# VectorE takes every score-decay product of the first twelve attention steps

## The chip, the cores and the metric

One core of one Trainium2 chip runs the whole kernel. The metric is the device time of one execution in microseconds (us); of several runs the median counts.

## The reference

A chunked linear attention with decay, then two feed-forward layers on its output. Cut to what matters:

```
for each chunk of the sequence:
    L = exp(cum_i - cum_j) * causal          # decays
    M = (C @ B.T) * L                        # scores times decays
    y = M @ x + (C @ state) * exp(cum)
    state = decay_full * state + sum(B x decay_from_j)
x = y, heads side by side                    # 3072 tokens x 256
x = max(x@w1, x@w2, x@w3) @ w_out            # hidden 768
out = (sigmoid(x@w_gate) * (x@w_val)) @ w_out2   # hidden 1536
```

The change touches the product `M`, the scores times the decays.

## The kernel before, in words

Attention is 64 steps: eight chunks c of 96 positions, and in each chunk eight groups g of four (batch, head) pairs; step k is c*8+g. A step makes its scores on TensorE (L280 for the first sixteen steps, L283 after) into a PSUM tile `s`, multiplies them by the decays into an SBUF tile `mt` (five buffers, used in turn), and multiplies that by `x` (L301) into a PSUM tile `y`, which also holds the state. The 16 state columns of `mt` are made by GpSimd (L288). The product itself is made in one of two ways: VectorE reads PSUM and writes `mt` (L295), or ScalarE copies PSUM to `mt` (L291) and GpSimd multiplies there (L292). After four steps ScalarE and VectorE evict `y` as a rounded high part and a low part (L310, L312) and VectorE transposes the state (L316).

A decay tile `dec` serves two steps; it has four buffers, is loaded by SyncE (L213) and turned into running products by two VectorE scans (L235). The load of tile n+4 into the buffer of tile n waits until both steps of tile n have used it.

The first feed-forward layer takes 512 tokens at a time (`t`). Twelve steps must be done for the first. Per hidden block m of 128 there are three products (`u_t_m_0`, `u_t_m_1`, `u_t_m_2`, six matmuls each, L350 to L352) in three PSUM banks, which they share with the scores `s`. ScalarE copies the first out (L395), VectorE takes the maximum with the second and the third (L397, L399), ScalarE and GpSimd split the result into `hi` and `lo` (L388, L390), and TensorE multiplies these into `o`. A bank is free for the next score or product only when it was read.

The weights of the first layer come as twelve loads named `raw_a00`, `raw_a01`, `raw_a10` to `raw_a51` (block, part). Each is decoded when it has landed: ScalarE L141, L144, L143, VectorE L148, L150, ScalarE L155, GpSimd L157. Most of these loads stand on SyncE's queue behind the load of a decay tile.

The order on each engine is not the written one. A scheduler with a timeline of its own sorts the instructions of each engine when the program is built; on the chip each engine then takes them in that order. So an edit of one step can move instructions of others.

Of the kernel before, what the change touches and what calls it, by code (L numbers as in the profile page):

```python
# [40 lines left out]
START = 12  # L41
# [25 lines left out]
def scan_attention_then_ffn(ctx: ExitStack, tc: tile.TileContext, xh, ah, bch, pick, bn, w1, w2, w3,  # L67
# [201 lines left out]
    def attention(k, ahead):  # L269

        c, g = steps[k]
        m = mt[k % MTS]
        if k < FIRST:
            ck = cm[:, k % MASKED]
            act.mul(ck.rearrange("p q i -> p (q i)"), bcf[c][:, BW:], pk[:, g:g + 1])
        ps = psu.tile([128, 4, 128], F32, tag="up", name=f"s{c}_{g}")
        for q in range(4):
            u = 4 * g + q
            if k < FIRST:
                pe.matmul(ps[:, q, 0:CH], bcf[c][:, 128 * q:128 * q + 128], ck[:, q],  # L280
                          start=True, stop=True)
            else:
                pe.matmul(ps[:, q, 0:CH], bi[c % 2][:, u, :], cs[c][:, u, :],  # L283
                          start=True, stop=True)
        for _ in range(ahead + 1):
            yield
        dc = dec[k // 2][:, 4 * (g % 2):4 * (g % 2) + 4]
        pool.tensor_tensor(out=m[:, :, CH:CH + N], in0=bx[c][:, 4 * g:4 * g + 4, :],  # L288
                           in1=dc[:, :, CH:LW].to_broadcast([128, 4, N]), op=ALU.mult)
        if k >= 4 and k % 2 == 0:  # L290
            act.copy(m[:, :, 0:CH], ps[:, :, 0:CH])  # L291
            pool.tensor_tensor(out=m[:, :, 0:CH], in0=m[:, :, 0:CH], in1=dc[:, :, 1:LW],  # L292
                               op=ALU.mult)
        else:
            last[0] = dve.tensor_tensor(out=m[:, :, 0:CH], in0=ps[:, :, 0:CH], in1=dc[:, :, 1:LW],  # L295
                                        op=ALU.mult)
        prepare(k)
        yield
        y = ys[g // 4]
        for q in range(4):  # L300
            pe.matmul(y[32 * q:32 * q + 32, g % 4, 0:CH + N], xs[c][:, 4 * g + q, :], m[:, q, :],  # L301
                      start=True, stop=True)
        if g % 4 == 3:
            yield
            h = g // 4
            o = (c * CP + 2 * CH * h) % RING
            src = y[:, :, 0:CH].rearrange("p (b k) i -> p b k i", k=KD)
            hi, lo = (v[:, :, o:o + 2 * CH].rearrange("p k (b i) -> p b k i", b=2)
                      for v in (xt_hi, xt_lo))
            act.copy(hi, src)  # L310
            yield
            dve.tensor_tensor(out=lo, in0=src, in1=hi.bitcast(F32), op=ALU.subtract)  # L312
            if c + 1 < NC:
                for q in range(4):
                    rows = slice(32 * q, 32 * q + 32)
                    dve.transpose(  # L316
                        out=xs[c + 1][rows, 16 * h:16 * h + 16, :].rearrange(
                            "p (g q) d -> p g q d", q=4)[:, :, q, :],
                        in_=y[rows, :, CH:128])

    def prepare(k):

        c, g = divmod(k, NG)
        if g == 0 and 0 < c < NC - 1:
            load_x(c + 1)
            splits.append(split_bc(c + 1))
        if splits and next(splits[0], None) is splits:
            splits.pop()
        n = k // 2
        if k % 2 == 0:  # L330
            if 5 <= n + 4 < NC * NP:
                load_decay(n + 4, ad)
        elif k < 9:
            decay(n + 1, n == 0)
        else:
            for i in ([n + 1] if k == 9 else []) + [n + 2]:
                if i < NC * NP:
                    with tc.issue_after(last[0].ins) if k > FIRST else ExitStack():
                        decay(i)

    def att_step(ahead=0):
        pipe.add(attention(done[0], ahead))
        done[0] += 1
# [236 lines left out]
```

## Time and profile before

| | |
|---|---|
| median of 3 runs | 581.4 us (580.17 to 582.3) |
| the profiled execution | 582.93 us |
| its span, first to last instruction | 581.1 us |
| TensorE busy | 560.9 us, 97% of the span |
| VectorE, ScalarE, GpSimd busy | 312.7, 260.7, 197.8 us |

The profiled execution is one run beside the three; 1.83 us of its time lie outside the span. Shares of busy time are means over stages with different limits: the attention start up to about 36 us, the stage in which the first layer's weights are decoded, and the rest.

### The profile page before, as it was taken

The numbers are of one execution on the slowest core, as the hardware profiler recorded it, in microseconds if no ns is written. First come the engines' busy times: TensorE is split into PE (matmuls) and PEld (weight loads), VectorE is DVE, ScalarE is ACT, GpSimd is POOL, SyncE is SP. The second block draws the span as 40 slices with busy tenths as digits, with TensorE's granted clock in tenths as the row PEclk, the third lists the DMA queues.
The fourth block names the chain that finished last, engine by engine and source line by source line (L and its number), as shares of the span: only waits on it lengthen the run. The fifth ranks groups of instructions, "written<-read, shape, count | busy, mean of one in ns | idle before, by whom it ended". The sixth has DMA issues, their size and how long they took to land.

```text
span 581.1 us, 8016 instructions
## 1 busy us (share of the span) xinstructions
PE 560.9 (97%) x2992; PEld 448.7 (77%) x2992; DVE 312.7 (54%) x455; ACT 260.7 (45%) x475; POOL 197.8 (34%) x219
## 2 busy tenths in 40 slices
PE   4988799999999999999999999999999999999997
PEld 4766567677777777788888888888888888888885
DVE  3879995655857754345766664243343333333332
ACT  4677645225344333256967675442333233232322
POOL 3566965427556523234665555310000000000000
PEclk9998999999999999999999999999999999999999
DMA  7999876827875800395000000010000001000000
GB/s 243 335 241 259 222 153 111 174 65 134 196 162 142 156 2 0 94 363 195 2 1 2 0 2 0 1 72 1 1 7 30 1 0 38 0 1 36 1 0 36
DMA packets 35366, 50.52 MB, mean 87 GB/s; under 512 B 3456, under 2 KB 24320, under 8 KB 35328
## 3 DMA queue, kind: packets, MB, share of 16 engines
q1 hardware_dynamic: 35328, 50.02, 33.4%
q8 instruction: 23, 0.38, 0.3%
q14 instruction: 15, 0.12, 0.1%
HBM read 38.51 MB, written 3.25 MB: 72 GB/s over the span
## 4 chain that ended last, share of the span: by engine, by line
PE 87%; DMA 6%; DVE 3%; issue 1%; SPq 1%; ACT 1%; POOL 0%; DVEq 0%; ACTq 0%; POOLq 0%
PE u L350 19%; PE u L351 18%; PE u L352 18%; PE o L351 8%; PE o L350 8%; PE o L352 8%; PE s L280 3%; PE y L301 3%; DMA raw_a<-in_w 3%; PE s L283 1%; DMA dec<-in_ah 1%; DMA cs<-parts 1%; DMA raw_a<-in_wo 1%; DVE dec L235 1%; SPq L252 0%
## 5 line engine op out<-in xcount | busy, mean ns | idle before, releaser
L388 ACT CAST hi<-s 128x512 fp32r<-128x512 f32 x108 | 67.1, 621 | 181.1 <-DVE s L406 132.1
L390 POOL TENSOR_TENSOR lo<-s,hi 128x512 fp32r<-128x512 f32 x60 | 80.9, 1348 | 95.3 <-ACT hi L388 92.3
L350 PE MATMUL u<-xt_hi,w_b 128*128 128x512 f32 x288 | 112.0, 389 | 0.0
L351 PE MATMUL u<-xt_lo,w_b 128*128 128x512 f32 x288 | 112.0, 389 | 0.0
L352 PE MATMUL u<-xt_hi,w_b 128*128 128x512 f32 x288 | 112.0, 389 | 0.0
L406 DVE TENSOR_TENSOR s<-u,s 128x512 f32<-128x512 f32 x72 | 49.6, 689 | 103.8 <-PE u L352 101.7
L350 PE MATMUL u<-xt_hi,w_a 128*128 128x512 f32 x216 | 89.1, 413 | 2.9 <-DVE s L399 2.0
L351 PE MATMUL u<-xt_lo,w_a 128*128 128x512 f32 x216 | 85.5, 396 | 0.1
L352 PE MATMUL u<-xt_hi,w_a 128*128 128x512 f32 x216 | 85.0, 394 | 0.0
L352 PEld LDWEIGHTS u<-xt_hi,w_b 128*128 128x128 f32 x288 | 54.1, 188 | 11.3
L350 PEld LDWEIGHTS u<-xt_hi,w_b 128*128 128x128 f32 x288 | 54.1, 188 | 11.2
L351 PEld LDWEIGHTS u<-xt_lo,w_b 128*128 128x128 f32 x288 | 54.0, 188 | 11.2
L235 DVE TENSOR_TENSOR_SCAN dec<-dec,delta 128x388 f32<-128x388 f32 x64 | 57.9, 945 | 1.7 <-DMA dec<-ad 1.5
L351 PE MATMUL o<-lo,w_b 128*128 128x512 f32 x144 | 56.1, 390 | 0.0
L352 PE MATMUL o<-hi,w_b 128*128 128x512 f32 x144 | 56.0, 389 | 0.0
L350 PEld LDWEIGHTS u<-xt_hi,w_a 128*128 128x128 f32 x216 | 41.2, 191 | 14.7 <-DVE s L399 2.5
L390 DVE TENSOR_TENSOR lo<-s,hi 128x512 fp32r<-128x512 f32 x48 | 33.2, 692 | 32.5 <-ACT hi L388 32.4
L352 PEld LDWEIGHTS u<-xt_hi,w_a 128*128 128x128 f32 x216 | 41.1, 190 | 9.1
L351 PEld LDWEIGHTS u<-xt_lo,w_a 128*128 128x128 f32 x216 | 41.1, 191 | 8.3 <-DVE xt_lo L312 0.6
L404 ACT ACTIVATE s<-u 128x512 f32<-128x512 f32 x72 | 43.1, 599 | 3.6 <-PE u L352 3.0
L350 PE MATMUL o<-hi,w_b 128*128 128x512 f32 x144 | 44.4, 390 | 0.1
L397 DVE TENSOR_TENSOR s<-u,s 128x512 f32<-128x512 f32 x36 | 24.8, 688 | 35.7 <-PE u L352 32.8
(60 smaller groups left out, 769.7 us busy)
## 6 DMA issues: line engine op xcount, KB each, us to landing
dec<-ad SPq DMA_DIRECT2D x30, 388.0 KB, 5.2
raw_a<-in_w SPq DMA_DIRECT2D x18, 256.0 KB, 7.2
bi<-parts SPq DMA_DIRECT2D x36, 128.0 KB, 5.3
cs<-parts SPq DMA_DIRECT2D x36, 96.0 KB, 5.2
xs<-in_xh SPq DMA_DIRECT2D x6, 512.0 KB, 4.5
raw_b<-in_wg SPq DMA_DIRECT2D x12, 256.0 KB, 5.8
raw_b<-in_wv SPq DMA_DIRECT2D x12, 256.0 KB, 5.8
raw_b<-in_wo SPq DMA_DIRECT2D x12, 256.0 KB, 5.8
```

The source lines that it names most:

```text
L235: dve.tensor_tensor_scan(out=f, data0=f, data1=delta.rearrange("p u w -> p (u w)"), initial=0.0, op0=ALU.mult, op1=ALU.add)
L280: pe.matmul(ps[:, q, 0:CH], bcf[c][:, 128 * q:128 * q + 128], ck[:, q], start=True, stop=True)
L283: pe.matmul(ps[:, q, 0:CH], bi[c % 2][:, u, :], cs[c][:, u, :], start=True, stop=True)
L301: pe.matmul(y[32 * q:32 * q + 32, g % 4, 0:CH + N], xs[c][:, 4 * g + q, :], m[:, q, :], start=True, stop=True)
L350: pe.matmul(ps, wlo, a_hi(k), start=k == 0, stop=False)
L351: pe.matmul(ps, whi, a_lo(k), start=False, stop=False)
L352: pe.matmul(ps, whi, a_hi(k), start=False, stop=k == kn - 1)
L388: act.copy(hl[0], s)
L390: eng.tensor_tensor(out=hl[1], in0=s, in1=hl[0].bitcast(F32), op=ALU.subtract)
L397: dve.tensor_tensor(out=s, in0=banks[1], in1=s, op=ALU.max)
L404: evict[0] = act.activation(out=s, in_=banks[0], func=AF.Sigmoid)
L406: evict[1] = dve.tensor_tensor(out=s, in0=banks[1], in1=s, op=ALU.mult)
```

## The change

```diff
-        if k >= 4 and k % 2 == 0:
+        if k >= START and k % 2 == 0:
             act.copy(m[:, :, 0:CH], ps[:, :, 0:CH])
             pool.tensor_tensor(out=m[:, :, 0:CH], in0=m[:, :, 0:CH], in1=dc[:, :, 1:LW],
                                op=ALU.mult)
         else:
             last[0] = dve.tensor_tensor(out=m[:, :, 0:CH], in0=ps[:, :, 0:CH], in1=dc[:, :, 1:LW],
                                         op=ALU.mult)
```

`START` is 12. So the products of steps 4, 6, 8 and 10 become one VectorE instruction each, in place of a ScalarE copy and a GpSimd product. From step 12 on nothing is edited. The built order changes on all five engines in about the first 120 us of the program, and not after it.

GpSimd, around steps 8 to 13. Before: the products of steps 8 and 10 (`mt3`, `mt0`) stand between the state columns of later steps.

```order
L288 TENSOR_TENSOR mt1_99<-bx1_156,dec5_216 128x4x16
L292 TENSOR_TENSOR mt3_101<-mt3_101,dec4_159 128x4x96
L288 TENSOR_TENSOR mt2_100<-bx1_156,dec6_248 128x4x16
L288 TENSOR_TENSOR mt3_101<-bx1_156,dec6_248 128x4x16
L292 TENSOR_TENSOR mt0_98<-mt0_98,dec5_216 128x4x96
L157 TENSOR_TENSOR w_a00_420<-r_a00_409,w_a00_420 128x512
```

The same place on GpSimd in the change:

```order
L288 TENSOR_TENSOR mt1_99<-bx1_156,dec5_216 128x4x16
L288 TENSOR_TENSOR mt2_100<-bx1_156,dec6_247 128x4x16
L157 TENSOR_TENSOR w_a00_416<-r_a00_405,w_a00_416 128x512
L288 TENSOR_TENSOR mt3_101<-bx1_156,dec6_247 128x4x16
L157 TENSOR_TENSOR w_a01_426<-r_a01_412,w_a01_426 128x512
```

Both products are gone, and the first weights' low part stands ahead of the state columns of step 13.

VectorE, around the product of step 17 (`mt2` from `s2_1`), which ends the use of the decay tile `dec8`. Before:

```order
L399 TENSOR_TENSOR s3_0_1_571<-u3_0_1_2_620,s3_0_1_571 128x512
L150 ISA r_a40_495<-t_a40_516,r_a40_495 128x1024
L295 TENSOR_TENSOR mt2_100<-s2_1_668,dec8_332 128x4x96
L235 SCALAR_TENSOR_TENSOR dec10_522<-dec10_522,delta_95 128x388 x2
L312 TENSOR_TENSOR xt_lo_93<-y1_104,xt_hi_92 128x2x2x96
L316 STREAM_TRANSPOSE xs2_324<-y1_104 32x4x32 x4
```

The same place on VectorE in the change:

```order
L150 ISA r_a40_491<-t_a40_512,r_a40_491 128x1024
L397 TENSOR_TENSOR s3_0_1_567<-u3_0_1_1_594,s3_0_1_567 128x512
L399 TENSOR_TENSOR s3_0_1_567<-u3_0_1_2_616,s3_0_1_567 128x512
L148 SCALAR_TENSOR_TENSOR t_a41_558<-raw_a41_520,sg1_88 128x512
L312 TENSOR_TENSOR xt_lo_93<-y1_104,xt_hi_92 128x2x2x96
L316 STREAM_TRANSPOSE xs2_321<-y1_104 32x4x32 x4
L295 TENSOR_TENSOR mt2_100<-s2_1_664,dec8_329 128x4x96
```

The decode of `raw_a41`, a low part and the transposes now stand ahead of the product of step 17.

ScalarE, around the copy of `u_0_3_0` out of its bank (L395 `s3_0_3`). Before:

```order
L388 CAST hi3_0_2_674<-s3_0_2_673 128x512
L395 COPY s3_0_3_769<-u3_0_3_0_772 128x512
L247 CAST parts3_661<-bc3_659 128x896
L291 COPY mt0_98<-s2_4_787 128x4x96
L155 CAST w_a50_650<-r_a50_616 128x512
L141 ACTIVATE sg1_88<-raw_a51_665 128x512
L144 ACTIVATE r_a51_706<-raw_a51_665 128x512
```

The same place on ScalarE in the change:

```order
L388 CAST hi3_0_2_670<-s3_0_2_669 128x512
L141 ACTIVATE sg1_88<-raw_a51_661 128x512
L144 ACTIVATE r_a51_702<-raw_a51_661 128x512
L395 COPY s3_0_3_765<-u3_0_3_0_768 128x512
L291 COPY mt0_98<-s2_4_783 128x4x96
L143 ACTIVATE raw_a51_661<-raw_a51_661 128x512
```

The first two decode instructions of the last load, `raw_a51`, now stand ahead of the two copies that free PSUM banks (of `u_0_3_0` and of the scores of step 20).

## Rows read from the trace of the kernel before

**Rows 1.** Busy time by stage: us, each engine's busy us, granted clock, DMA share.

```profile
36.00:78.00 42.00, 34.61 (x228) 25.52 (x229) 40.80 (x54) 28.93 (x51) 33.50 (x31) 0.96 1.00 243
78.00:100.00 22.00, 21.95 (x138) 15.79 (x136) 14.67 (x28) 9.60 (x19) 11.71 (x14) 1.00 0.54 120
```

**Rows 2.** Timeline of TensorE, end of the start: start us, us, what.

```profile
27.58 3.73 PE L280 MATMUL s<-y 128*128 128x96 f32 x16
...
36.52 0.98 PE L301 MATMUL y<-mt,xs 128*32 128x112 f32 x16 [1.45 <-POOL mt L292]
38.19 0.76 PE L350 MATMUL u<-xt_hi,w_a 128*128 128x512 f32 x1 [0.69 <-ACT xt_hi L310]
```

**Rows 3.** Timeline of VectorE in the same stretch.

```profile
34.27 0.56 DVE L295 TENSOR_TENSOR mt<-s,dec 128x384 f32<-128x384 f32 x1 [2.30 <-PE s L280]
...
37.13 1.12 DVE L148 SCALAR_TENSOR_TENSOR t_a<-raw_a,sg 128x512 int32<-128x512 int32 x1
```

**Rows 4.** Groups of GpSimd, 15 to 36 us: busy, mean ns, idle before.

```profile
L292 POOL TENSOR_TENSOR mt<-mt,dec 128x384 f32<-128x384 f32 x4 | 4.2, 1045 | 0.0
```

**Rows 5.** What TensorE waited for, 34 to 95 us: total, times, longest.

```profile
PE u L350 <- DVE s L399: 1.6, 1, 1.6
PE s L283 <- DVE s L399: 1.6, 1, 1.6
...
PE s L283 <- DVE s L397: 1.0, 1, 1.0
```

**Rows 6.** Timeline of VectorE around the product of step 17 (L295).

```profile
62.66 0.54 DVE L295 TENSOR_TENSOR mt<-s,dec 128x384 f32<-128x384 f32 x1
...
64.85 0.53 DVE L312 TENSOR_TENSOR xt_lo<-y,xt_hi 128x384 fp32r<-128x384 f32 x1
65.29 1.28 DVE L316 STREAM_TRANSPOSE xs<-y 32x128 f32<-32x128 f32 x4
...
67.21 1.51 DVE L148 SCALAR_TENSOR_TENSOR t_a<-raw_a,sg 128x512 int32<-128x512 int32 x1
```

**Rows 7.** Timeline of ScalarE, 71 to 78 us.

```profile
71.12 0.62 ACT L155 CAST w_a<-r_a 128x512 fp32r<-128x512 f32 x1 [3.00 <-DVE r_a L150]
...
72.73 0.57 ACT L395 COPY s<-u 128x512 f32<-128x512 f32 x1
...
77.34 0.79 ACT L141 ACTIVATE sg<-raw_a 128x512 f16<-128x512 f32 x1
78.00 0.64 ACT L144 ACTIVATE r_a<-raw_a 128x512 int32<-128x512 uint32 x1
```

**Rows 8.** SyncE's DMA issues: the decay tile, then the second half of `raw_a51`.

```profile
65.64 0.52 SPq L213 DMA_DIRECT2D dec<-ad  x1
...
67.86 0.33 SPq L127 DMA_DIRECT2D raw_a<-in_wo  x1
```

**Rows 9.** DMA issues of 67.5 to 69 us: KB each, us to landing.

```profile
raw_a<-in_wo SPq DMA_DIRECT2D x1, 256.0 KB, 8.4
```

**Rows 10.** All loads of the first layer's weights.

```profile
DMA to landing us min/median/max: 4.0/7.3/9.9
```

**Rows 11.** SyncE's issue of the two halves of `raw_a40`.

```profile
45.46 1.93 SPq L127 DMA_DIRECT2D raw_a<-in_w  x2
```

**Rows 12.** Timeline of TensorE: first matmul of `u_0_1_1`, `u_0_3_2`, two output steps, `u_0_4_2`.

```profile
54.01 0.48 PE L350 MATMUL u<-xt_hi,w_a 128*128 128x512 f32 x1
...
74.10 0.40 PE L350 MATMUL u<-xt_hi,w_a 128*128 128x512 f32 x1
...
75.56 0.59 PE L301 MATMUL y<-mt,xs 128*32 128x112 f32 x16
...
82.98 0.48 PE L350 MATMUL u<-xt_hi,w_a 128*128 128x512 f32 x1
```

**Rows 13.** TensorE by stretch: us, busy, granted clock, DMA share.

```profile
46.00:49.00 3.00, 2.05 (x20) 1.00 1.11 165
...
50.00:53.00 3.00, 3.00 (x14) 0.50 1.12 246
```

## Prediction

> **What bounds the kernel now.** I read the busy time by stage first. From 78 us on TensorE is busy without a gap worth naming: 21.95 of 22 us in the first stretch of it [rows 1]. The built order is the same again after about 120 us, so whatever the change does has to show as an earlier or later arrival of TensorE at that unbroken stretch. Between 36 and 78 us it is not TensorE that decides: VectorE is busy 40.80 of 42 us there, TensorE 34.61, and the DMA engines work at a share of 1.00 [rows 1]. This is the stage in which the first layer's weights land and are decoded. Then I read TensorE's timeline at the end of the start stage: it waits 1.45 us for a GpSimd product and 0.69 us for the high part before the first layer matmul at 38.19 [rows 2]. Last, the list of TensorE's waits: the large ones behind 38 us are 1.6, 1.6 and 1.0 us, all for a VectorE instruction that frees a PSUM bank [rows 5]. So the change meets two limits: a wait at 35 us that it takes away, and a stage that lives on when banks come free.
>
> **The wait that goes.** Up to 34 us TensorE runs two score steps in 3.73 us and two output steps in 0.98 [rows 2]. In the new order scores and outputs alternate: from 27.58 three score steps (3 x 1.87 = 5.6) and two output steps (0.98), with 0.3 more since they follow each other one by one, end at 34.5; four output steps (1.9) end at 36.4; the high part's copy takes about 0.5. The first layer matmul comes at 36.9 in place of 38.19, **1.3 us earlier**, if VectorE keeps up. It has to make four products more, 0.56 us each, 2.2 in all. Before, it stood idle for 2.30 us ahead of step 11's product [rows 3]; that idle time began at 31.97. Into it now go the products of steps 8 and 10 (1.1) and a low part and transposes, which were moved ahead (0.53 + 1.28 where they stand later [rows 6]): step 11's product starts at 34.9 and ends at 35.4, before TensorE's fourth output step needs it at 35.9. Steps 4 and 6 lie earlier, where VectorE waited for decay tiles. So the four products cost nothing; without that idle time they would cost their 2.2. The decode that stood at 37.13 [rows 3] now follows a 0.6 us instruction behind 35.4, at about 36.0: VectorE is 1.2 ahead. Bounds of this term: 2.1 (both waits gone) and 0 (VectorE late).
>
> What ScalarE and GpSimd lose is four copies of about 0.5 and four products of 1.045 [rows 4]. Neither engine is on the path at 17 to 36 us but for the one wait already counted. The Trainium skill (SBUF — State Buffer, Who interferes with whom) says that a VectorE instruction with two SBUF inputs contends with a GpSimd instruction that reads SBUF. By that rule the sum would gain up to another 4.2 us, the whole of the four products. The rows give nothing of it: the VectorE instructions beside them ended in idle time anyhow, so I take 0.
>
> **What the new order moves.** The scheduler believes that weights land earlier than they do, and puts their decode ahead of instructions that free banks. The place that I think decides is ScalarE at 72 us. Before, it copies `u_0_3_0` out of its bank at 72.73 and begins to decode `raw_a51` at 77.34 [rows 7]. In the change the first two decode instructions of `raw_a51` stand ahead of that copy. They can't start before the load has landed.
>
> When does it land? Its second half was issued at 67.86, 2.2 us behind the decay tile at 65.64 [rows 8], and took 8.4 us [rows 9]: 76.3. In the change the decay tile must wait for the product of step 17, which before ended at 63.2 [rows 6]. That product is now behind a decode (1.51), a low part (0.53) and transposes (1.28) [rows 6], 3.3 together, less VectorE's 1.2: it ends at 65.3. So the decay tile goes out at 65.3 and the load at 67.5. For its landing I take the median of all twelve, 7.3 us; the ends are 4.0 and 9.9 [rows 10], and its own 8.4 lies between. It lands at 74.8. ScalarE then needs 0.66 and 0.64 for the two instructions and 0.57 for the copy [rows 7]: 76.7. TensorE's `u_0_3_2`, which needs one of the two banks behind that wait, started at 74.10 [rows 12]: **2.6 us later**.
>
> Some of it comes back. From `u_0_3_2` to `u_0_4_2` TensorE took 8.9 us (74.10 to 82.98) [rows 12], with the 1.0 us wait for L397 inside [rows 5]; in the change that wait is over by then. The two output steps at 75.56 (0.59) [rows 12] now stand ahead, and one later step has come in: 0.3 less. So 7.6 us behind 76.7, `u_0_4_2` starts at 84.3, 1.3 late, and the step that came in (0.3) is work done: **1.0 us late**. That holds VectorE's and TensorE's head start already, since both were spent in the landing time above.
>
> Then the clock. TensorE would be idle for some 3 us before `u_0_3_2`. Before, it was busy 2.05 of 3 us from 46 to 49 us, and from 50 on the granted clock was 0.50, its 1.2 GHz level, for 3 us [rows 13]. Half of 3 us is 1.5 us lost. I take the 1.5, since the new gap is longer than those; the other bound is 0. Sum: +1.0 +1.5 = **+2.5 us**. The profiled execution took 582.93 and would take 585.4; against the median of 581.4, which the time is compared with, that is **583.9 us**. A half per cent of it is 2.9 us, about what a measurement of this kernel can tell from no change.
>
> The rule that speaks against the change is in the Trainium skill (PSUM — Partial Sum Buffer, Engine vs sequencer instructions): ScalarE's queue is strictly first in, first out. In the trace ScalarE idled 3.00 us for a VectorE decode at 71.12 and copied `u_0_3_0` only behind it, at 72.73 [rows 7]. By the rule the sum is the one above; if ScalarE could pass a waiting instruction, the copy would stay near 72.7 and the head start alone would be left, 580.1.
>
> **The rivals.**
>
> *The holds add up* (slower). The same thing stands earlier on ScalarE: the decode of `raw_a40` is ahead of the copy of step 14's scores, the bank that `u_0_1_1` waits for. The second half of `raw_a40` was issued before 47.4 [rows 11]; at 7.3 us [rows 10] it lands at about 54, and 1.3 + 0.5 us of ScalarE later the bank is free at 55.8, where `u_0_1_1` started at 54.01 [rows 12]. Add the 1.2 GHz level behind the gap, and block 1 is some 2 to 3 us late. My 65.3 leaves that out. If step 17's product, which stands behind block 1's evictions, ends 2 us later, then the decay tile, `raw_a51` and `u_0_3_2` do too: 585.9. The same comes of a landing of 9.3 instead of 7.3. For it: everything in 36 to 78 us is tight, and the DMA share is 1.00 [rows 1]. Against it: VectorE's 1.2 us lead. It decides once step 17's product ends behind 65.7, since 0.4 us more put the time over the half per cent.
>
> *The head start stands* (faster). `raw_a51` lands in 4 to 5 us, as the fastest loads do [rows 10], at about 72; then the copy is no later than before, the waits of 1.6 and 1.0 us [rows 5] stay or shrink, and 1.3 us are kept: 580.1. If VectorE's lead also removes the two waits of 1.6, it is 576.9. Against it: its own row says 8.4 [rows 9].
>
> *The head start is eaten and nothing else happens.* VectorE is busy 97% of the stage, and what decides there is its total work, which is the same at the end of the stage in both orders: 581.4.
>
> **How the numbers follow.** I give my forecast 0.42, the added holds 0.30, the kept head start 0.14, and no change 0.14. Within the forecast the landing (7.3 or 8.4) and the clock (0 or 1.5) spread the time over 582.4 to 585.0, a fifth of it (0.09) over the half per cent of 584.3. So slower is 0.30 + 0.09, about 0.39. Faster by 2.9 us needs the head start and both waits: 0.07. The rest, 0.54, is within. The range goes from 579.9 (head start kept) to 586.5 (added holds and a little more); it leaves out the best end of the one and the worst of the other.
>
> **What would show it.** In the profile of the changed kernel the wait of TensorE for L292 before 37 us is gone and the first L350 starts near 36.9. VectorE shows little idle time from 31 to 37 us. ScalarE shows an idle stretch ending with L141, with the landing of a weight load as its cause, shortly before the copy L395 at about 76, and TensorE a gap of about 3 us before it, then a granted clock near 0.5. If instead TensorE goes from 70 to 78 us with no gap over 1.5 us, the step on ScalarE's order is wrong; if the gap is there and `u_0_4_2` starts before 83, the step on what comes back is wrong. A first layer matmul later than 38 us would show that VectorE did not have the time for the four products.

## The result and the profile after

The changed kernel takes 587.83 us (median of 4 executions, 585.41 to 589.16), the kernel before 581.33 (580.17 to 582.3): a ratio of 1.0108, 95% interval 1.007 to 1.0146. It is slower by 6.5 us, where 2.5 were forecast, and lies above the range.

The profiled execution took 589.16 us with a span of 587.4. The start comes first: TensorE's timeline (start us, us, what, idle time and what ended it).

```profile
24.75 1.10 PE L280 MATMUL s<-y 128*128 128x96 f32 x8 [1.06 <-DVE mt L295]
...
30.72 1.99 PE L280 MATMUL s<-y 128*128 128x96 f32 x8 [4.54 <-ACT raw_a L143]
...
35.83 0.77 PE L350 MATMUL u<-xt_hi,w_a 128*128 128x512 f32 x1 [0.68 <-ACT xt_hi L310]
```

The wait for GpSimd's product is gone and the first layer matmul starts at 35.83 instead of 38.19 [rows 2]. A wait of 4.54 us that nobody forecast stands at 26 us. The row names L143, but the scores of step 11 take the bank of step 8's, which VectorE's new product frees: that product starts at 30.04, on VectorE's queue behind a decode, a low part, the transposes and two scans. A bank whose reader was ScalarE now waits for its turn on VectorE.

Then the stage in which the weights are decoded (engines' busy us, granted clock, DMA share):

```profile
36.00:78.00 42.00, 33.75 (x197) 24.33 (x198) 36.02 (x48) 28.23 (x50) 30.14 (x28) 0.86 0.99 230
78.00:100.00 22.00, 22.00 (x125) 16.00 (x124) 13.85 (x25) 7.65 (x15) 10.40 (x12) 0.92 0.31 90
```

VectorE, busy 40.80 us there before [rows 1], is busy 36.02: the engine that bounds the stage idles 4.8 us more. Its timeline and ScalarE's say where:

```profile
72.02 0.61 ACT L388 CAST hi<-s 128x512 fp32r<-128x512 f32 x1
75.87 0.78 ACT L141 ACTIVATE sg<-raw_a 128x512 f16<-128x512 f32 x1 [3.24 <-DMA raw_a<-in_wo]
76.52 0.63 ACT L144 ACTIVATE r_a<-raw_a 128x512 int32<-128x512 uint32 x1
77.05 0.57 ACT L395 COPY s<-u 128x512 f32<-128x512 f32 x1
```

```profile
77.65 0.69 DVE L397 TENSOR_TENSOR s<-u,s 128x512 f32<-128x512 f32 x1 [4.30 <-ACT s L395]
78.62 0.95 DVE L148 SCALAR_TENSOR_TENSOR t_a<-raw_a,sg 128x512 int32<-128x512 int32 x1 [0.27 <-DMA dec<-ad]
...
82.10 0.69 DVE L399 TENSOR_TENSOR s<-u,s 128x512 f32<-128x512 f32 x1
```

ScalarE stands still 3.24 us for `raw_a51`, with the copy of `u_0_3_0` behind it (77.05 instead of 72.73 [rows 7]); VectorE's next eviction needs that copy, and stands still 4.30 us. SyncE sent the decay tile when it was forecast (65.16) and the load 1.3 us earlier than that (66.24), and the chain that ended last in 60 to 80 us runs through that load:

```profile
65.16 0.34 SPq L213 DMA_DIRECT2D dec<-ad  x1
...
66.24 0.33 SPq L127 DMA_DIRECT2D raw_a<-in_wo  x1
```

```profile
66.24 9.55 DMA raw_a<-in_wo
...
77.15 0.48 ACT s L395
77.63 0.04 issue
77.67 0.50 PE u L350
```

On TensorE the gap is 3.34 us, the granted clock in 78 to 84 us is 0.72, and `u_0_4_2`, at 82.98 before [rows 12], comes at 86.97:

```profile
77.67 0.50 PE L350 MATMUL u<-xt_hi,w_a 128*128 128x512 f32 x1 [3.34 <-ACT s L395]
...
86.97 0.50 PE L350 MATMUL u<-xt_hi,w_a 128*128 128x512 f32 x1
```

```profile
78.00:84.00 6.00, 6.00 (x32) 0.72 0.26 96
```

From 93 us on every later copy (L395 and L404) of this execution is 3.5 us later than in the profile of before, up to 193 us. There another 2.8 us are lost, in a part whose order is the same in both kernels: VectorE waits 1.14 us for a decay tile, TensorE 1.15 us and 0.47 behind it, and the clock falls.

```profile
198.97 1.81 DVE L235 TENSOR_TENSOR_SCAN dec<-dec,delta 128x388 f32<-128x388 f32 x2 [1.14 <-DMA dec<-ad]
```

```profile
203.20 0.33 PE L283 MATMUL s<-cs,bi 96*128 96x96 bf16 x4 [1.15 <-DVE s L397]
204.00 0.50 PE L350 MATMUL u<-xt_hi,w_a 128*128 128x512 f32 x1 [0.47 <-DVE s L399]
```

As far as the profiles show, that second loss belongs to the execution and not to the change: of the eighteen profiles below one has it in full (the first, 2.8 us, whose execution took 584.74 where its kernel's median is 580.99) and the others at most 0.7. The three other executions of the changed kernel have no profile.

### The profile page after: what moved, and what is told of

Read it like the earlier page. It is cut to its first block, busy times and chain, and to the rows that moved or that the text cites. A ratio compares the mean times of both kernels' runs of the same rounds, so it can differ in the third digit from the quotient of the medians.

```text
span 587.4 us, 8017 instructions
## 1 busy us (share of the span) xinstructions
PE 557.4 (95%) x2992; PEld 444.6 (76%) x2992; DVE 313.4 (53%) x459; ACT 259.0 (44%) x471; POOL 192.6 (33%) x215
## 4 chain that ended last, share of the span: by engine, by line
PE 82%; DMA 13%; DVE 2%; SPq 1%; issue 1%; ACT 1%; DVEq 0%; ACTq 0%
PE u L350 19%; PE u L351 18%; PE u L352 18%; PE o L351 8%; PE o L350 8%; PE o L352 8%; DMA raw_a<-in_w 5%; DMA raw_a<-in_wo 2%; PE y L301 2%; DMA dec<-ad 1%; DMA bi<-parts 1%; PE s L283 1%; DMA bc<-in_bch 1%; DMA xs<-in_xh 1%; DVE dec L235 1%
## 5 line engine op out<-in xcount | busy, mean ns | idle before, releaser
L350 PE MATMUL u<-xt_hi,w_a 128*128 128x512 f32 x216 | 89.8, 416 | 7.0 <-ACT s L395 4.0
L351 PE MATMUL u<-xt_lo,w_a 128*128 128x512 f32 x216 | 87.0, 403 | 0.0
L352 PE MATMUL u<-xt_hi,w_a 128*128 128x512 f32 x216 | 86.6, 401 | 0.0
L235 DVE TENSOR_TENSOR_SCAN dec<-dec,delta 128x388 f32<-128x388 f32 x64 | 57.8, 945 | 2.1 <-DMA dec<-ad 1.9
L397 DVE TENSOR_TENSOR s<-u,s 128x512 f32<-128x512 f32 x36 | 24.8, 688 | 43.3 <-PE u L352 36.2
L404 ACT ACTIVATE s<-u 128x512 f32<-128x512 f32 x72 | 43.1, 598 | 3.7 <-PE u L352 3.1
```

The source lines that it names most:

```text
L235: dve.tensor_tensor_scan(out=f, data0=f, data1=delta.rearrange("p u w -> p (u w)"), initial=0.0, op0=ALU.mult, op1=ALU.add)
L350: pe.matmul(ps, wlo, a_hi(k), start=k == 0, stop=False)
L351: pe.matmul(ps, whi, a_lo(k), start=False, stop=False)
L352: pe.matmul(ps, whi, a_hi(k), start=False, stop=k == kn - 1)
L397: dve.tensor_tensor(out=s, in0=banks[1], in1=s, op=ALU.max)
L404: evict[0] = act.activation(out=s, in_=banks[0], func=AF.Sigmoid)
```

## The experiments

The order of the built program can be set by hand: each experiment lists the first instructions of every engine and chains them by edges that fix the order and wait for nothing.

```diff
+    for name, rows in ORDER.items():
...
+        for a, b in zip(rows, rows[1:]):
+            tc.add_manual_dep(traced[b], traced[a].name, edge, reason="order")
...
         scan_attention_then_ffn(tc, *args)
+        in_order(tc)
```

So products and order can be changed apart. In the table, "slower by" is the median less the median of the kernel before in the same session; the interval is that of the ratio. The last three columns come from ScalarE's timeline: how much later than in the second profile of before (the control: 61.64, 69.76 and 90.57 us) the copy L395 of block 2, of block 3 and of the first block of the second 512 tokens starts.

| | median us | slower by | ratio, 95% | block 2 | block 3 | next t |
|---|---|---|---|---|---|---|
| the profile of before | 582.93 (one) | | | +2.9 | +3.0 | +3.0 |
| changed kernel | 587.83 | 6.5 | 1.007 to 1.0146 | +4.4 | +7.3 | +6.4 |
| e1 new products, old order | 580.99 | 0.5 | 0.9999 to 1.0037 | +2.0 | +2.1 | +2.0 |
| e2 old products, new order | 588.71 | 8.2 | 1.0122 to 1.017 | +4.8 | +7.1 | +7.3 |
| e3 a51 behind copy (ScalarE) | 584.1 | 3.6 | 1.0048 to 1.0114 | +4.0 | +3.2 | +4.1 |
| e4 before, a51 ahead of copy | 585.44 | 5.0 | 1.0062 to 1.0117 | -0.3 | +5.2 | +5.3 |
| e5 new head, old tail | 581.22 | 0.1 | 0.9989 to 1.002 | +2.0 | +2.1 | +2.1 |
| e6 old head, new tail | 588.76 | 7.6 | 1.0091 to 1.017 | +4.5 | +8.1 | +7.2 |
| e7 before, evictions first | 582.53 | 1.4 | 1.0008 to 1.0043 | +0.4 | +1.3 | +1.8 |
| e9 a51 behind, both engines | 586.02 | 5.4 | 1.0073 to 1.0138 | +5.2 | +3.5 | +9.1 |
| e10 early evictions first | 587.08 | 6.5 | 1.0083 to 1.013 | +5.0 | +8.6 | +6.7 |
| e11 a51 loaded early | 583.75 | 3.2 | 1.0035 to 1.0074 | +4.7 | +5.9 | +4.5 |
| e12 before, a51 loaded early | 580.71 | 0.1 | 0.9984 to 1.0016 | +1.1 | +1.1 | +1.2 |
| e13 new order on VectorE only | 592.64 | 11.8 | 1.0165 to 1.0226 | +4.7 | +8.7 | +14.4 |
| e14 new order but on ScalarE | 598.62 | 17.8 | 1.0285 to 1.0329 | +8.9 | +13.2 | +18.6 |
| e15 ScalarE, VectorE old | 591.3 | 10.5 | 1.0142 to 1.0219 | +6.0 | +5.8 | +12.5 |
| e16 new up to block 2 | 583.6 | 3.0 | 1.0009 to 1.0069 | +3.6 | +2.7 | +4.4 |
| e17 old up to block 2 | 585.39 | 4.8 | 1.0051 to 1.015 | +3.6 | +6.3 | +4.4 |
| e18 new up to block 1 | 580.52 | -0.1 | 0.9985 to 1.0022 | +0.5 | +0.1 | +0.1 |

**Products and order apart (e1, e2).** e1 keeps the edit's products and gives all other instructions the order of before; e2 keeps the order of the change and gives back the ScalarE copies and GpSimd products.

> The four products are VectorE's as in the changed kernel, but every other instruction of all five engines stands in the order of the kernel before. Theory H (the hold: the loss comes from the order alone, from raw_a51's decode standing ahead of the copy of u_0_3_0 on ScalarE): the products cost nothing, time within 1.5 us of 581.3, no TensorE gap over 1.5 us at 70 to 78 us. Theory B (a score bank now stays taken until VectorE's product, and TensorE, starved at 26 to 31 us, falls to the 1.2 GHz level until 44 us): a TensorE gap of 3 us or more ahead of the scores of step 11, granted clock near 0.50 from 34 to 44 us, first eviction of the layer 1.5 us or more late, time 584 or more. Theory C (the loss lies in the unedited stretch at 200 us): neither; a gap of TensorE at about 200 us that comes and goes.

> The four products are made as in the kernel before (ScalarE copy, GpSimd product), but all other instructions stand in the order of the changed kernel. Theory H: TensorE waits 2.5 us or more for the copy of u_0_3_0 at about 74 us, and the time is 584.5 to 588, as in the changed kernel. Theory B: no gap of 4 us at 26 to 31 us, granted clock 1.00 from 34 to 44 us; the head start of the alternating order (first layer matmul near 36) survives, time 580 to 582.5. Theory C: like either, with or without a gap at about 200 us.

The four products cost 0.5 us (the interval is 0 to 2.1 us); the order alone costs all of the loss, a little more than theory H had for e2. Theory B is out by both times.

**One hold, taken away and put in (e3, e4).** e3 edits ScalarE's order in the changed kernel:

```order
 L388 CAST hi3_0_2_670<-s3_0_2_669 128x512
+L395 COPY s3_0_3_765<-u3_0_3_0_768 128x512
+L291 COPY mt0_98<-s2_4_783 128x4x96
 L141 ACTIVATE sg1_88<-raw_a51_661 128x512
 L144 ACTIVATE r_a51_702<-raw_a51_661 128x512
-L395 COPY s3_0_3_765<-u3_0_3_0_768 128x512
-L291 COPY mt0_98<-s2_4_783 128x4x96
```

e4 is its mirror in the kernel before:

```order
 L388 CAST hi3_0_2_674<-s3_0_2_673 128x512
+L141 ACTIVATE sg1_88<-raw_a51_665 128x512
+L144 ACTIVATE r_a51_706<-raw_a51_665 128x512
 L395 COPY s3_0_3_769<-u3_0_3_0_772 128x512
```

> The changed kernel with one edit of its order: on ScalarE the first two decode instructions of raw_a51 stand behind the copies of u_0_3_0 and of step 20's scores, as before the change. Theory H: TensorE's gap of 3.34 us ahead of u_0_3_2 shrinks under 1 us, the low clock at 78 to 84 us goes with it, u_0_4_2 starts 2.5 to 4 us earlier than 86.97, and the time falls by 2.5 to 4 us to 583.5 to 585.5. Theory B: gap gone as well but the time falls by less than 1.5 us, since what stands late stays late. Theory C: 587, or 584.5 where the gap at 200 us is missing.

> The kernel before with one edit of its order: on ScalarE the first two decode instructions of raw_a51 stand ahead of the copies of u_0_3_0 and of step 20's scores, as in the changed kernel. Theory H: raw_a51 lands at about 76.3, the copy follows at 77.6, u_0_3_2 starts 3 to 4 us later than 74.10 with the 1.2 GHz level behind the gap; time 584 to 586. Theory B: the gap is there but most of it comes back in waits that were there before (1.6 and 1.0 us for VectorE), time 581 to 583. Theory C: 581.3 but for a gap at 200 us.

The hold by itself costs 5.0 us in the kernel before (interval 3.6 to 6.8 us), with block 2 still in time (-0.3) and block 3 late (+5.2). ScalarE and VectorE in e4:

```profile
73.81 0.77 ACT L141 ACTIVATE sg<-raw_a 128x512 f16<-128x512 f32 x1 [4.18 <-DMA raw_a<-in_wo]
...
74.99 0.56 ACT L395 COPY s<-u 128x512 f32<-128x512 f32 x1
```

```profile
75.58 0.69 DVE L397 TENSOR_TENSOR s<-u,s 128x512 f32<-128x512 f32 x1 [2.59 <-ACT s L395]
78.57 0.69 DVE L399 TENSOR_TENSOR s<-u,s 128x512 f32<-128x512 f32 x1 [2.29 <-PE u L352]
```

VectorE idles twice, 4.9 us together, for the copy and then for the product that TensorE could start only behind it. In e3 the copy is in time at 72.95, but 3.6 us stay; its intervals and those of the changed kernel overlap, so e3 alone doesn't size the hold. VectorE in e3 shows why part of it stays: its own decode of `raw_a51`, ahead of the eviction L399 of block 3, now waits.

```profile
77.56 0.69 DVE L148 SCALAR_TENSOR_TENSOR t_a<-raw_a,sg 128x512 int32<-128x512 int32 x1 [3.01 <-ACT raw_a L143]
...
80.78 0.69 DVE L399 TENSOR_TENSOR s<-u,s 128x512 f32<-128x512 f32 x1
```

**Where in time (e5, e6).** The lists of all engines are cut at the first layer matmul.

> VectorE's four products; up to the first matmul of the first layer all engines take their instructions in the order of the changed kernel, and behind it in the order of the kernel before. Theory H2 (the order costs its time behind the first layer matmul: decode ahead of evictions, on ScalarE for u_0_3_0 and on VectorE for block 0 and 1): time within 1.5 us of the kernel before, though the gap of some 4.5 us at 26 to 31 us and the 1.2 GHz level behind it are there. Theory B (that gap and the low clock): 583.5 or more, the first eviction of the layer 1.5 us or more late and never made up.

> VectorE's four products; up to the first matmul of the first layer the order of the kernel before, behind it the order of the changed kernel. Theory H2: 4.5 to 8 us slower than before, with TensorE's gap of 3 us ahead of u_0_3_2 and waits of 1.5 us or more for evictions by VectorE at 48 to 54 us. Theory B: less than 3 us slower.

The new head is worth nothing either way; the new tail costs everything. The profiled execution of e5 does not test the gap at 26 us: its score steps took 2.02 us from 15 us on, and TensorE had no gap there. The profile of e18, which has the same head, shows a gap of 3.16 us ahead of a score step of 1.99 us, and e18 took as long as the kernel before (-0.1).

**Evictions first, in the kernel before (e7), and the control (e8).** e7 edits VectorE's order, here for block 2 (and likewise L399 of block 1, L397 and L399 of block 3):

```order
 L397 TENSOR_TENSOR s3_0_2_673<-u3_0_2_1_710,s3_0_2_673 128x512
+L399 TENSOR_TENSOR s3_0_2_673<-u3_0_2_2_731,s3_0_2_673 128x512
 L148 SCALAR_TENSOR_TENSOR t_a41_562<-raw_a41_524,sg1_88 128x512
 L150 ISA r_a41_552<-t_a41_562,r_a41_552 128x1024
-L399 TENSOR_TENSOR s3_0_2_673<-u3_0_2_2_731,s3_0_2_673 128x512
```

> The kernel before (old products, old order) with one edit: on VectorE four evictions of blocks 1 to 3 (L399 of block 1 and 2, L397 and L399 of block 3) are moved ahead of the decode instructions that stand between them and the eviction before. Theory H2 (an eviction behind decode costs what TensorE waits for it, also in the kernel before): the waits of 1.6, 1.6 and 1.0 us go, the time falls by 2 to 4 us to 576.5 to 578.5. Rival T (VectorE is busy 97% of that stage, its total decides and the order does not): within 1 us of the kernel before. Rival D (what the decode loses, TensorE waits for later, as a weight that is not ready): slower by 0.5 to 2 us, with new waits of L350 for L155 or L157.

> The kernel before with its own order written out, the way in which the other experiments set theirs: the same instructions in the same order. All theories: the time of the kernel before within its spread, 579 to 583. Its trace is a second profile of the kernel before: it shows whether TensorE's half-speed matmuls up to 42 us are in every execution.

e7 gained nothing (slower by 1.4 us, interval 0.5 to 2.5, so rival T's 1 us is not excluded). Theory H2 failed here and rival D's figure held: the waits for evictions went, and others came, though for products, low and high parts rather than for weights, as TensorE's list of 36 to 84 us shows (total, times, longest).

```profile
PE u L350 <- DVE mt L295: 2.4, 2, 2.0
PE u L351 <- DVE xt_lo L312: 2.4, 1, 2.4
PE o L350 <- ACT hi L388: 2.3, 1, 2.3
```

The control took 579.95 us and is 3.0 us ahead of the first profile of the same program from block 2 on. Its first layer matmul starts at 34.54, not at 38.19 [rows 2], and it has a gap in the start too, 2.66 us for a ScalarE copy of scores, where the first profile has none:

```profile
20.21 1.13 PE L280 MATMUL s<-y 128*128 128x96 f32 x8
...
24.33 3.73 PE L280 MATMUL s<-y 128*128 128x96 f32 x16 [2.66 <-ACT mt L291]
...
28.90 2.02 PE L280 MATMUL s<-y 128*128 128x96 f32 x8
...
34.54 0.79 PE L350 MATMUL u<-xt_hi,w_a 128*128 128x512 f32 x1 [0.70 <-POOL w_a L157]
```

**Chasing the rest on single engines (e9, e10).** e9 adds to e3 VectorE's half; e10 moves L397 and L399 of blocks 0 and 1 ahead of the decode next to them, in the same way as e7.

```order
 L397 TENSOR_TENSOR s3_0_3_765<-u3_0_3_1_788,s3_0_3_765 128x512
-L148 SCALAR_TENSOR_TENSOR t_a51_719<-raw_a51_661,sg1_88 128x512
-L150 ISA r_a51_702<-t_a51_719,r_a51_702 128x1024
 L312 TENSOR_TENSOR xt_lo_93<-y0_103,xt_hi_92 128x2x2x96
```

> The changed kernel with two edits of its order: raw_a51's first two decode instructions behind the copies of u_0_3_0 and of step 20's scores on ScalarE (as in the third experiment), and its two on VectorE behind the eviction L399 of block 3 and the product of step 21. Theory H3 (the whole loss is VectorE's idle time for this one late load: with ScalarE's hold gone VectorE itself waited 3.01 us for it, ahead of that eviction): VectorE has no idle time over 1 us at 70 to 80 us, time 580.5 to 582.5. Theory V (evictions of blocks 0 and 1 stand behind decode on VectorE; 1.5 and 1.8 us of TensorE's waits at 50 to 54 us): within 1 us of the third experiment, 583 to 585.

> The changed kernel with one edit of its order on VectorE: the evictions L397 and L399 of blocks 0 and 1 are moved ahead of the decode instructions next to them; raw_a51 stays where the change put it. Theory V: TensorE's waits of 1.5 and 1.8 us for these go, time 583 to 585. Theory H3: block 2 comes earlier, but block 3 still waits for raw_a51's landing; within 1.5 us of the changed kernel's 587.8.

e9 missed both theories' figures (its profiled execution took 589.44, the other three about 586); in e10 the time is that of theory H3, but block 2 did not come earlier as it had said. In e9 the low part L312 became VectorE's next instruction, and the copy that it needs (L310) stands behind `raw_a51`'s decode on ScalarE; in e10 the waits for VectorE turned into waits for ScalarE's copies of scores. VectorE's waits in e9 at 62 to 84 us, then TensorE's in e10 at 36 to 84:

```profile
DVE xt_lo L312 <- ACT xt_hi L310: 5.0, 1, 5.0
```

```profile
PE u L350 <- ACT mt L291: 4.9, 3, 2.2
PE u L350 <- ACT s L395: 3.1, 1, 3.1
```

**The load instead of its decode (e11, e12).** SyncE's order, in the changed kernel (e11) and likewise in the kernel before (e12, shown); the edge that ties these two loads to the decay tile is left out.

```order
 L127 DMA raw_a50_589<-in_w2 128x2x256
+L127 DMA raw_a51_665<-in_w3 128x2x256
+L127 DMA raw_a51_665<-in_wo1 128x512
 L224 DMA xs3_655<-in_xh 128x1024
 L252 DMA bi1_97<-parts3_661 16x8x512 x3
 L252 DMA cs3_662<-parts3_661 16x8x384 x3
 L213 DMA dec12_663<-ad_105 128x776
-L127 DMA raw_a51_665<-in_w3 128x2x256
-L127 DMA raw_a51_665<-in_wo1 128x512
```

> The changed kernel with one edit of SyncE's order: the two loads of raw_a51 stand directly behind those of raw_a50, ahead of the decay tile of steps 24 and 25 and of the loads between. They go out at about 58 us in place of 66, and land at about 66 to 68. Theory H3: nothing waits for them any more, time 580 to 582.5. Theory V: the gap at 74 us goes, 583 to 585. Rival Q (the DMA engines are at a share of 1.1 there, so what goes out earlier makes others late, and VectorE waits for the decay tile or the third chunk's scores instead): 585 or more.

> The kernel before (old products, old order) with the same edit of SyncE's order: raw_a51's two loads directly behind raw_a50's. In the kernel before VectorE waits 1.1 us at 78 us. Theory H3: up to 1 us faster, 580 to 581.3. Rival Q: slower by 1 to 3 us.

In e11 nothing waits for the load any more, with the decode where the change put it: ScalarE goes on without a gap at 74.48. It idles 3.93 us at 72.60, for a decode by VectorE, as it did before the change for 3.00 [rows 7].

```profile
74.48 0.80 ACT L141 ACTIVATE sg<-raw_a 128x512 f16<-128x512 f32 x1
75.14 0.65 ACT L144 ACTIVATE r_a<-raw_a 128x512 int32<-128x512 uint32 x1
75.69 0.57 ACT L395 COPY s<-u 128x512 f32<-128x512 f32 x1
```

That gives 3.3 of the 6.5 us back (6.5 less 3.2; the two intervals just touch), so theory H3, which wanted all of it, falls. The figure is theory V's, whose mechanism e10 leaves without support. In the kernel before the same move changes nothing.

**Which engine (e13 to e15).** The list of each engine is that of the one or the other kernel.

> VectorE's four products; VectorE takes its instructions in the order of the changed kernel, the other four engines in the order of the kernel before. Theory S (the loss stands in ScalarE's order: one decode after another ahead of evictions, each waiting for its load or for VectorE): within 2.5 us of the kernel before. Theory W (VectorE's order alone): 4 us slower or more. Theory G (no engine alone: where one engine's order has decode first the hold moves to it): between, 2 to 5 us slower.

> VectorE's four products; ScalarE takes its instructions in the order of the kernel before, the other four engines in that of the changed kernel. Theory S: within 1.5 us of the kernel before. Theory W: 4 us slower or more. Theory G: 2 to 5 us slower, with VectorE's decode of raw_a51 as the wait in place of ScalarE's.

> VectorE's four products; ScalarE and VectorE take their instructions in the order of the kernel before, TensorE, GpSimd and SyncE in that of the changed kernel. Theories S, W and G: within 1.5 us of the kernel before, since the engines that evict have the old order. Theory P (TensorE's new order, with scores ahead of products): 3 us slower or more.

All three are worse than either whole order. Theory W's open figure (4 us or more) fits e13 and e14, but it wanted e15 within 1.5 us; theory P's fits e15 and says nothing of the other two. I read them as one thing: the lists of the engines belong together, and a mix makes one engine wait for another's later instruction. In e14 VectorE waits 13.5 us for ScalarE's decode in 36 to 100 us:

```profile
DVE t_a L148 <- ACT raw_a L143: 13.5, 6, 4.3
```

So they say nothing on which engine the loss belongs to.

**Cuts at blocks 1 and 2 (e16 to e18).** As e5 and e6, cut at the first matmul of block 2 or block 1.

> VectorE's four products; all engines in the order of the changed kernel up to the first matmul of block 2 (61.5 us), behind it in the order of the kernel before. Theory J (two places add up: some 3.2 us in blocks 0 and 1, as the run with raw_a51's load ahead left them, and some 3.7 us in blocks 2 and 3 with raw_a51): 2.5 to 4 us slower than the kernel before. Theory K (what is late at block 2 is slack that VectorE makes up; the loss is all behind it): within 1.5 us.

> VectorE's four products; all engines in the order of the kernel before up to the first matmul of block 2, behind it in the order of the changed kernel, with raw_a51's decode ahead of the copy of u_0_3_0. Theory J: 3 to 4.5 us slower than the kernel before. Theory K: 6 to 8 us slower.

> VectorE's four products; the order of the changed kernel up to the first matmul of block 1 (50 us), behind it that of the kernel before. Theory J, if its first place is block 0 (the first eviction L395 behind the decode of raw_a20 and raw_a30, L397 behind that of raw_a21 and the next): 2.5 to 4 us slower; if it is block 1: within 1.5 us. Theory K: within 1.5 us.

Theory J's figures came out, with e17 a little over: up to block 1 (50 us) the new order costs nothing, between the two cuts some 3.0 us, behind the second 4.8. The two sum to 7.8, where the whole new tail cost 7.6 (e6). The intervals are wide, 0.5 to 4.0 us for e16 and 3.0 to 8.7 for e17, and do not exclude theory K by themselves; e11, with 3.2 us left, speaks for J.

The 4.8 us are not the hold of `raw_a51` alone. In e17 the first matmul of block 2 is 0.5 us later than in the control (59.14 against 58.61), but the copy of `u_0_2_0` 3.6: between L310 and this copy ScalarE takes L141, L144 and L143 twice, where in the control it takes L141 and L144 once. In the changed kernel's profile 1.50 us of idle time for a load stand there too (64.25).

e16 and e18 part at block 1, and TensorE's waits in 46 to 62 us differ there, first e16, then e18:

```profile
PE s L280 <- DVE s L399: 1.9, 1, 1.9
```

```profile
PE s L280 <- DVE s L399: 0.3, 1, 0.3
```

In e16 VectorE has a decode and the two scans of a decay tile (L235, 1.80 us) ahead of L399 of block 0, in e18 the decode alone.

No run beat the kernel before clear of the noise.

## Why the prediction was wrong, step by step

- **The wait that goes** (first layer matmul 1.3 us earlier). Against the one profile it came 2.4 us earlier (35.83), but the control of the old order starts at 34.54: the start's duration differs more between executions than by the change. e5 gives the head start its value: none (0.1 us). This is the first step that failed, and the sum went by it: without VectorE's 1.2 us the decay tile and all behind it would have come 1.2 later and the sum would have been 3.7. The step also took TensorE's 1.87 us per score step for the new order, where it took 1.10 up to 26 us and 1.99 behind the gap, and it missed that a product on VectorE holds a bank that ScalarE had freed early.
- **The four products cost nothing.** Right: e1, 0.9999 to 1.0037. The rule of the Trainium skill (SBUF — State Buffer, Who interferes with whom) would have given up to 4.2 us for GpSimd's relief; e1 shows no gain, so 0 was the right value to take here.
- **ScalarE's hold.** Right in mechanism, and nearly in its numbers, which is in part luck: the decay tile went out at 65.16 (65.3 forecast), the load at 66.24 (67.5), landed behind 9.55 us (7.3) at 75.8 (74.8), and `u_0_3_2` came at 77.67 (76.7). The load left 1.3 us early and took 2.2 longer; and the decay tile, in time against the first profile (65.64), is 2.4 us late against the control (62.74). The Trainium skill (PSUM — Partial Sum Buffer, Engine vs sequencer instructions) has ScalarE's queue strictly first in, first out; the trace agrees, with 3.24 us of idle time ahead of a copy whose product was done at about 70.9.
- **"Some of it comes back", and the clock.** Both held. The forecast gave TensorE 7.6 us from `u_0_3_2` to `u_0_4_2` and 1.5 for the clock, 9.1 together; it took 9.3 (77.67 to 86.97), and 0.72 of the clock in 78 to 84 us is 1.7 us lost. What the step left out is VectorE, which bounds this stage: it stands still 4.30 us for the copy, and behind the hold it has decode, low part and transposes ahead of L399 of block 3 (82.10). Without the head start the forecast for the hold is 3.7; e4 measured 5.0, with 3.7 inside its interval, so its size is not shown to be wrong.
- **The first of the holds.** The rival *the holds add up* came nearest (585.9): a second place, ahead of block 2, costs 3.0 us (e16, 1.0009 to 1.0069). My sum put it at nothing, on VectorE's 1.2 us lead, and this is the second step that failed: the 1.2 us of the lead and these 3.0 make 4.2, where 6.5 exceeds 2.5 by 4.0; the intervals allow no closer sum. The wait isn't quite the one that I named: in the changed kernel `raw_a40` had landed when ScalarE came to it at 51.74, and in e16 ScalarE waited only 0.86 us for it (54.64). But the place is real: with VectorE's evictions out of the way (e10), TensorE waits 2.23 us at 53.53 for the copy of step 14's scores, which stands behind that decode. Which instructions make these 3.0 us between 50 and 61 us is not settled. e10 shows that moving VectorE's evictions alone gains nothing; that ScalarE's and VectorE's lists both have decode ahead there, so that one edit moves the wait to the other engine, is argued from e9, e10 and e14, not shown by a run that frees both.
- **The execution compared with.** I worked out the change against one profile and moved the result to the median by the 1.5 us between their times. That profile was itself 3.0 us late from block 2 on (control); its start ran at the lower clock level (last section). Against it the changed kernel's shows +3.5 us at 93 us, 1.0 more than forecast; against the control +6.4, near the 6.5 of the medians, though the control's execution was itself 1.2 us faster than its session's median. A sum of 2.5 us from one profile of each stage was smaller than what two profiles of one kernel differ by.

## What to carry to other kernels

When a scheduler with a timeline of its own sorts the program, a one-line edit is an edit of every engine's order: price the order by itself, by pinning the old one. Find the engine that bounds the stage and count its idle time, since a hold on an idle engine (ScalarE) can be lost nearly whole when the bounding engine (VectorE) waits for it: 4.9 us of idle time and 5.0 us in e4. Where the program is late already less was lost: in the changed kernel's profile the copies go from 4.4 us behind the control at block 2 to 6.4 at the next 512 tokens, with 4.30 us of idle time between. Where a late load causes the hold, moving its decode (e3) handed the wait to the next instruction that depends on it, and moving the load (e11) left no wait for it; their times, 3.6 and 3.2 us slower, are not told apart. And compare two profiles of the old kernel before a difference of a few us is read from one.

## What the runs showed of the hardware that was not expected

The granted clock of a row can say 1.00 while the matmuls take as long as at the lower of the two levels (1.2 and 2.4 GHz). Before, score steps at 27.58 us took 1.87 us each [rows 2], and the row of that stretch says 1.00 (first fence, of before); in the changed kernel they took 1.10 at 22.25 with 1.00, and 1.99 at 30.72 with 0.50 (second and third fence).

```profile
24.00:36.00 12.00, 11.07 (x83) 1.00 0.90 233
```

```profile
22.25 1.10 PE L280 MATMUL s<-y 128*128 128x96 f32 x8 [0.45 <-DVE mt L295]
```

```profile
12.00:24.00 12.00, 9.90 (x112) 1.00 1.01 348
30.00:36.00 6.00, 4.04 (x41) 0.50 1.10 263
```

In the control, which is the same program as the kernel before, a score step took 1.13 us at 20.21 and 2.02 us at 28.90. So the level in the start differs between executions of one program, and in the start it is read from durations rather than from the row.

The level in the start goes with the time of the whole execution. The profiles of the kernel before, e1, e5, e12 and e18 all have the old order from block 1 on, e12 but for one load. In the first four the score steps from 15 us on took 1.87 to 2.02 us, and the copy of the next 512 tokens came 1.2 to 3.0 us later than in the control; in e18 they took 1.10 to 1.13 us up to 22 us, and it came 0.1 later. Executions without a profile fit: of the 14 of the kernel before beside e1, five have a mean granted clock of 0.991 to 0.997 and took 581.16 to 581.79 us, nine have 0.973 to 0.985 and took 579.06 to 580.86. The higher reading goes with the longer time, as it would where it leaves out a start at the lower level; in three other sessions a few executions of the second kind are as long as the first. Why an execution starts at one level or the other, no run shows.
